# The first block's transfers through DRAM: outer steps of 16, 32 or 64 partitions over rows of 1 KB, and all spills ahead of the three fills

## The chip, the core and the metric

The kernel runs on one core of a Trainium2 chip. The metric is the device time of one execution in microseconds (us). The core has a matrix engine (TensorE, PE in the profile), three elementwise engines (VectorE = DVE, ScalarE = ACT, GpSimd = POOL) and 16 DMA engines, which all DMA queues share. DMAs are issued here by SyncE (SP) and by ScalarE; "SPq" and "ACTq" in the profile are the issuing instructions. Each engine works through its own instructions in order, and an issuing engine that waits on a semaphore holds up everything behind it.

## The reference

The input is a batch of 8 sequences of 3008 rows by 256 features. A two-dimensional Fourier transform is taken of each, its real part kept, and every row then goes through a two-layer network with 2048 hidden features.

```
X = np.fft.fft(x, axis=1)
X = np.fft.fft(X, axis=2)
x = X.real.reshape(B * S, D)
h = x @ w_in
g = h * (1.0 / (1.0 + np.exp(-1.702 * h)))
return g @ w_out
```

## The kernel before

A sequence is transformed in two stages, with 3008 = 47 x 64. Stage one multiplies, for each of 64 residues, 47 rows by a table of cosines and sines; stage two combines the residues. Between the two the data change layout: stage one leaves a frequency on a partition, stage two needs the residue there. The kernel does that through DRAM: a "spill" writes stage one's rows to a scratch tensor, a "fill" reads them back into the tile `t4` with another assignment of rows to partitions. The feature transform is folded into the weights. After stage two, the network runs in steps: 8 sequences, 3 blocks each, 16 steps a block, almost all of it on PE.

The first sequence has a path of its own, in a setup of some 120 us, since nothing can be hidden behind earlier work. It goes as follows, in the order written out by hand.

- `load_first` and `load_mirror` bring in the first sequence; a loop over `i` from 0 to 7 folds it on DVE (`fold_first`), multiplies on PE (`mix_first`, line 335) and copies the result on ACT (line 337) into one of four tiles `made[0]` to `made[3]`, two values of `i` for each tile. A tile has two halves c, at partitions 0 and 64; in each half the first 16 partitions belong to the first of stage two's three blocks.
- `spill_first(k, engines)` (line 343) writes those 16 partitions of both halves of `made[k]` to the scratch tensor `Tf`: two DMAs of 16 partitions by four rows of 1 KB, 64 KB each. Half 0 goes on SP's queue; half 1 goes on ACT's queue, but for k = 2, where both go on SP's.
- `fill_first` (line 347) reads `Tf` back into `t4`, in three DMAs, all on SP's queue: partitions 1, 3, 5 and so on (64 of them, 256 KB, called fill 1 below), partitions 2, 6, 10 and so on (32 of them, 128 KB, fill 2), and partitions 0, 4, 8 and so on (32, 128 KB, fill 3). Fill 1 needs the spills of k = 0 and 1, fill 2 those of k = 2, fill 3 those of k = 3.
- Each row that a fill moves is 4 KB, all four of a partition's values in one piece. For that the table `w0` has its first 16 columns of every residue reordered, and the scratch tensor is written so that the four values stand side by side. On the DRAM side a fill's access pattern begins with a step of 4, on the SBUF side with a step of 64 or 32 partitions.
- `spill_rest` (line 352) writes the other 32 frequencies to another scratch tensor, `Td`; `fill(0, 4, NG)` (line 374) reads them much later, for the other two blocks.

Once `t4` is filled, `rotate(0, 0, 4)` works on one column of it with PE (tile `psr`, line 196), `stage2(0, 0)` multiplies it on PE (line 394), DVE transposes the result (line 401), and `first_row(0)` follows on PE and ACT (tile `psf`, lines 532 and 533).

Meanwhile the weights are prepared. They arrive as 64-bit numbers in eight loads of 1 MB (`load_in`, line 427, and `load_out`, line 432), and each goes through ACT (`sizes`, line 445, and `low`, line 455), POOL (`clamp`, line 451), DVE (`high`, lines 470 and 471) and POOL again (lines 483 and 491). `load_in(0)` is on SP's queue, `load_in(1)` on ACT's, issued when i is 5; `load_out(0)` and the others are on SP's queue, after the three fills. In ACT's own order, `sizes` of `out0` comes after `first_row(0)`.

SP's order around the change, before: the two halves of `load_in(0)`, the small matrices (line 904), the spills of k = 0 and 1, fill 1, the two spills of k = 2, the spill of k = 3, fills 2 and 3, `load_out(0)`, `spill_rest`. The DMAs of SP and ACT use eight completion counters in turn, so a DMA also waits until the one issued eight places before it, in the order of the program, has landed.

Of the kernel before, what the change touches and what calls it, by code (L numbers as in the profile page):

```python
# [27 lines left out]
F32 = mybir.dt.float32  # L28
# [7 lines left out]
NJ = NB // 2  # L36
NM = 48
# [10 lines left out]
def view(ap, offset, *dims):  # L48
    return bass.AP(ap.tensor, ap.offset + offset, [list(d) for d in dims])
# [6 lines left out]
def kp(u, a):  # L56

    n, i = a // 4, 2 * (a % 4) + u
    return 8 * n + i if n else 7 - i


def tables(S, D):

    assert S == NA * NB and D == 256
    H = D // 2
    ks = np.array([kp(u, a) for a in range(NG) for u in range(NU)])
    s = NB * np.arange(NA)[:, None, None] + np.arange(NB)[None, :, None]
    angle = 2.0 * np.pi * ((s * ks) % S) / S
    cos, sin = np.cos(angle), np.sin(angle)
    w1 = np.zeros((NA, NJ + 3, NG * NU, 2))  # L70
    w1[:, 1:NJ, :, 0], w1[:, 1:NJ, :, 1] = cos[:, 1:NJ], sin[:, 1:NJ]
    e0, o0, e1, o1 = ENDS
    w1[:, e0, :, 0], w1[:, o0, :, 0], w1[:, e1, :, 1], w1[:, o1, :, 1] = cos[:, 0], sin[:, 0], cos[:, NJ], sin[:, NJ]


    w0 = np.zeros((128, NJ + 1, NG * NU, 2))
    low, high, back = w0[0:2 * NA:2], np.zeros((NA, NJ + 1, NG * NU, 2)), NJ - np.arange(1, NJ)
    low[:] = w1[:, :NJ + 1]
    high[:, 1:NJ, :, 0], high[:, 1:NJ, :, 1] = cos[:, NJ + back], -sin[:, NJ + back]
    high[:, e0, :, 1], high[:, o0, :, 1] = cos[:, NJ], -sin[:, NJ]  # L80
    w0[33:33 + 2 * NA:2] = high
    w0 = w0.reshape(128, NJ + 1, NM)
    w0[:, :, :16] = w0[:, :, :16].reshape(128, NJ + 1, 4, 4).swapaxes(2, 3).reshape(128, NJ + 1, 16)
    sign = np.ones((128, 4))
    sign[33:33 + 2 * NA:2] = -1.0

    c, q = np.divmod(np.arange(NJ), 16)
    m2 = []
    h, y = np.array([0, 2, 1, 3])[np.arange(NJ) % 4], np.arange(NJ) // 4
    at = 16 * (y // 4) + 4 * h + y % 4  # L90
    for jj in np.where(c, 16 + q, np.where(q, 16 - q, 0))[at], 4 * (q // 2) + 2 * (q % 2) + c:
# [12 lines left out]

    m, d = np.arange(D)[:, None], np.arange(H)[None, :]
    phi = 2.0 * np.pi * ((m * d) % D) / D
    cd = np.stack([np.cos(phi), -np.sin(phi)], 1)
    cd[:, 1, 0] = 1.0 - 2.0 * (np.arange(D) % 2)
    cd = cd.reshape(2, H, 2, NB, 2).transpose(1, 0, 2, 4, 3)
    small = [t.reshape(128, -1) for t in (*m2, rot, cd)]  # L110
    pad = 64 - NM
    ends = 2.0 * np.pi * ((NJ * np.arange(NM)[:, None] * ks) % S) / S
    w1 = np.pad(w1[:, :NJ + 1], ((0, NM - NA), (0, 0), (0, 0), (0, 0)))
    w1[:, 0], w1[:, NJ] = 0.0, 0.0
    for c in range(2):
# [8 lines left out]
def kernel(ctx: ExitStack, tc, x, w_in, w_out, tab1, tab2, out):  # L124
    nc = tc.nc
    B, S, D = x.shape
# [16 lines left out]
    Xr = [nc.dram_tensor(f"Xr{b}", (NA, NJ, D), F32, kind="Internal").ap() for b in range(B)]  # L143
    Nd = nc.dram_tensor("Nd", (B * NBLK, 512), F32, kind="Internal").ap()
    Tk = nc.dram_tensor("Tk", (B * NBLK * NF, 1), F32, kind="Internal").ap()
    Tf = nc.dram_tensor("Tf", (NJ * 4, 4 * D), F32, kind="Internal").ap()
    Td = [nc.dram_tensor(f"Td{b}", (NG * 128, D), F32, kind="Internal").ap() for b in range(B)]

    w1 = const.tile([128, (NJ + 1) * NM + 64 - NM], F32, tag="w1", name="w1")
# [48 lines left out]
    t4t, pqt, nbt = {}, {}, {}  # L198
# [112 lines left out]
    def fold_first(g):  # L311

        t, e = xt[:, 4 * g:4 * g + 4, :], room[g]
        fwd, rev = t[:, :, 1:H], free(t, D - 1, [D, 4], [-1, H - 1])
        nc.vector.tensor_tensor(e[:, :, 0:H - 1], fwd, rev, op=ALU.subtract)
        if g not in BY_PE:
            nc.vector.tensor_tensor(fwd, fwd, rev, op=ALU.add)

    def mix_first(i):

        ps, ns = bank("ps1"), (2 * i + 2, 2 * i + 1) if i < 7 else (0, 15)
        for at, n in enumerate(ns):
            todo = [], []
            for c, slot in enumerate((n, NJ - n if n else 16)):
                o = ps[64 * c:64 * c + 64, at * D:(at + 1) * D]
                even, odd_ = (w[:, k * NM:k * NM + 64] for w, k in ((w0, slot), (odd, slot or NJ)))
                todo[c].append((o[:, H + 1:], odd_, room[slot // 4][:, slot % 4, 0:H - 1], True, True))
                folded = slot // 4 not in BY_PE
                todo[c].append((o[:, 0:H + 1], even, xt[:, slot, 0:H + 1], True, folded))
                if not folded:  # L330
                    todo[c].append((o[:, 1:H], even, free(xt[:, slot], D - 1, [-1, H - 1]), False, True))
            for k in range(3):
                for c in range(2):
                    for o, w, rhs, first_, end in todo[c][k:k + 1]:
                        nc.tensor.matmul(o, lhsT=w, rhs=rhs, start=first_, stop=end, skip_group_check=True)
        to = 2 - i % 2 * 2
        nc.scalar.copy(made[i // 2][:, to:to + 2, :].rearrange("p j d -> p (j d)"), ps[:])

    PLACE = 3, 1, 2, 0

    def spill_first(k, engines):
        for c, eng in enumerate(engines):
            eng.dma_start(out=view(Tf, (PLACE[k] + 16 * c) * 16 * D, [D, 16], [64 * D, 4], [1, D]), in_=made[k][64 * c:64 * c + 16])

    def fill_first(at, apart):
        one, n = t4t[0][at:at + 1], NJ // apart
        nc.sync.dma_start(out=bass.AP(one.tensor, one.offset, [[apart * t4t[0][:].ap[0][0], 4 * n], [1, 4 * D]]),
                          in_=view(Tf, at * 16 * D, [4 * D, 4], [apart * 16 * D, n], [1, 4 * D]))

    def spill_rest(k):  # L350
        for c in range(2):
            nc.sync.dma_start(out=view(Td[0], (NJ * 16 + 16 * c + PLACE[k]) * D, [NJ * D, NM - 16], [4 * D, 4], [1, D]),
                              in_=made[k][64 * c + 16:64 * c + NM])

    def load_matrices():
# [514 lines left out]
    odd, w0 = flat[:, 0:n0], flat[:, 6176:6176 + n0 + 4]  # L870
# [4 lines left out]
    made = rooms[1:] + [pqp.tile([128, 4, D], F32, tag="pq", name="e")[:]]  # L875
# [5 lines left out]
    for lo, hi in (28, 32), (24, 28), (20, 24), (8, 12), (12, 20):  # L881
# [10 lines left out]
                      in_=view(tab1, 0, [tab1.shape[1], 128], [28 * NM, 2], [1, ends]))  # L892
# [16 lines left out]
    for i, need in enumerate(((0, 7), (1,), (6,), (2,), (5,), (3,), (4,), ())):  # L909
        for g in need:  # L910
            fold_first(g)
        mix_first(i)
        if i == 0:
            warm(3)
            spare[:] = spare[5:] + spare[:5]
        if i % 2:
            spill_first(i // 2, (nc.sync, nc.sync if i == 5 else nc.scalar))
        if i == 5:
            load_in(1, nc.scalar)
        if i == 3:  # L920
            fill_first(1, 2)
        if i == 7:
            fill_first(PLACE[2], 4)
        if i == 3:
            sizes(in0, nc.scalar, 0, 512)
            clamp(in0, 0, 512)
        if i in (4, 7):
            low(in0, 512 * (i // 7), 512)
        if i == 6:
            sizes(in0, nc.vector, 512, 512)  # L930
            clamp(in0, 512, 512)
            for h0 in (0, 512):
                high(in0, h0, 512)
    fill_first(PLACE[3], 4)
    load_out(0, nc.sync)
    spill_rest(0)
    load_in(2, nc.sync)
    for k in range(1, 4):
        spill_rest(k)
# [35 lines left out]
    n = len(steps)  # L975
# [17 lines left out]
    for b in range(B):  # L993
# [43 lines left out]
    for t in range(n + LAG):  # L1037
# [14 lines left out]
        else:  # L1052
# [13 lines left out]
            one, other = (t - LAG, (1, 2, 4, 7)), (t - LAG - 1, (5, 6, 3))  # L1066
# [70 lines left out]
```

## Time and profile before

| | us |
|---|---|
| median of three runs | 1852.49 |
| lowest and highest | 1852.17 and 1854.78 |
| the profiled execution's own time | 1852.52 |
| its span in the trace | 1850.7 |
| PE busy | 1827.8 (99% of the span) |
| DVE, ACT, POOL busy | 1481.1, 1138.7, 997.7 |
| HBM read and written | 65.07 MB and 48.05 MB, 61 GB/s over the span |

Between the span and the execution's own time lie 1.8 us. Times in the trace count from the span's start. The profile's chain of waits follows the work that ended last back to the start, each piece to what released it. In the view of stages, a row gives the length of a stretch, then for each engine its busy time and the instructions in it, then the granted clock of TensorE (1.00 is full), the mean busy share of the 16 DMA engines, and GB/s. In the timeline, a row has start, length, engine, line, operation and count, and in brackets how long the engine had been idle and what ended that.

### The profile page before, as it was taken

The page shows a single profiled execution, that of the slowest core. Times are in us where ns is not written, and L with a number is a line of the kernel's source. Part 1 is how long each engine was busy: PE and PEld are TensorE (multiplying, and loading weights), DVE is VectorE, ACT ScalarE, POOL GpSimd, SP SyncE. Part 2 cuts the span into 40 slices and gives each one's busy share as a digit, 9 for nine tenths or more (in the row PEclk, how much of TensorE's full clock was granted, in tenths as well). Part 3 has the DMA queues.
Part 4 walks back from the last instruction along what each step waited for, and adds up shares of the span by engine and source line. Part 5 has one row for each costly group of instructions (what it writes and reads, how often), then busy time and mean ns, then how long its engine had stood idle before and what let it go on. Part 6 is the DMA issues. An engine that isn't in the chain of part 4 may idle for free.

```text
span 1850.7 us, 55846 instructions
## 1 busy us (share of the span) xinstructions
PE 1827.8 (99%) x23650; PEld 1399.4 (76%) x23650; DVE 1481.1 (80%) x1930; ACT 1138.7 (62%) x2231; POOL 997.7 (54%) x1068
## 2 busy tenths in 40 slices
PE   7999999999999999999999999999999999999998
PEld 4677777777777777777777777777777877778776
DVE  5888888887888878887888778877888788878874
ACT  3656665666567666666665666666666666556663
POOL 3695556654556546565455644656446654444442
PEclk8999999999999999999999999999999999999999
DMA  8731340213312142211512115021241111100001
GB/s 250 204 72 32 80 74 22 61 26 92 62 28 55 37 107 37 60 32 36 114 20 66 35 51 98 19 74 27 65 79 24 36 26 56 30 19 13 23 19 24
DMA packets 151605, 105.95 MB, mean 57 GB/s; under 512 B 106193, under 2 KB 132819, under 8 KB 150796
## 3 DMA queue, kind: packets, MB, share of 16 engines
q1 hardware_dynamic: 148140, 99.35, 22.5%
q8 instruction: 186, 3.05, 0.7%
q10 hardware_dynamic: 3216, 3.03, 0.6%
q14 instruction: 63, 0.52, 0.1%
HBM read 65.07 MB, written 48.05 MB: 61 GB/s over the span
## 4 chain that ended last, share of the span: by engine, by line
PE 93%; POOL 2%; DVE 2%; DMA 2%; issue 1%; ACT 0%; SPq 0%; DVEq 0%; POOLq 0%; ACTq 0%
PE x L196 34%; PE o L196 26%; PE low L717 25%; PE o L717 4%; PE ps L273 2%; PE ps L394 1%; DMA xt<-in_x_dram 1%; DMA Tf<-big 1%; POOL wo L491 0%; PE po L196 0%; DMA t<-Tf 0%; DVE big L471 0%; POOL wo L509 0%; POOL wst L483 0%; POOL big L648 0%
## 5 line engine op out<-in xcount | busy, mean ns | idle before, releaser
L648 POOL TENSOR_TENSOR big<-big 128x256 f32<-128x256 f32 (+1 forms) x376 | 352.7, 938 | 786.0 <-ACT big L640 666.2
L196 PE MATMUL x<-pq,wcs 128*64 128x256 f32 (+1 forms) x6016 | 768.8, 376 | 1.3 <-ACT g L630 0.8
L196 PE MATMUL o<-big,wo 128*64 128x256 f32 (+1 forms) x4800 | 621.1, 375 | 0.5 <-DVE big L655 0.5
L196 PEld LDWEIGHTS x<-pq,wcs 128*64 128x64 f32 x6016 | 414.3, 137 | 180.7 <-issue 15.6
L630 ACT ACTIVATE g<-x 128x512 f32<-128x512 f32 (+1 forms) x376 | 221.7, 590 | 380.3 <-PE x L196 379.2
L196 PEld LDWEIGHTS o<-big,wo 128*64 128x64 f32 x4800 | 341.5, 137 | 147.1 <-DVE big L655 0.9
L649 POOL TENSOR_TENSOR big<-big 128x256 f32<-128x256 f32 (+1 forms) x376 | 411.3, 1094 | 0.0
L637 DVE TENSOR_TENSOR big<-g,x 128x512 f32<-128x512 f32 (+1 forms) x376 | 250.9, 667 | 182.3 <-ACT big L633 182.0
L618 ACT ACTIVATE x<-nb,af 128x256 f32<-128x256 f32 (+1 forms) x752 | 353.0, 469 | 70.4 <-DVE pq L401 57.3
L717 PE MATMUL low<-big 128*64 128x128 f32 (+1 forms) x5888 | 381.4, 270 | 0.0
L717 PEld LDWEIGHTS low<-big 128*64 128x64 f32 x5888 | 336.8, 137 | 28.2
L633 ACT ACTIVATE big<-x 128x512 f32<-128x512 f32 (+1 forms) x376 | 219.2, 583 | 120.4 <-PE x L196 110.4
L679 DVE TENSOR_TENSOR big<-big 128x1024 f32<-128x1024 f32 (+1 forms) x184 | 235.5, 1280 | 65.6 <-PE low L717 42.8
L640 ACT ACTIVATE big<-big 128x512 f32<-128x512 f32 (+1 forms) x376 | 231.6, 616 | 35.7 <-DVE big L637 33.4
L717 PE MATMUL low<-big,wo 128*64 128x128 f32 (+1 forms) x2944 | 220.2, 270 | 0.1
L681 DVE TENSOR_TENSOR big<-big 128x512 f32<-128x512 f32 (+1 forms) x184 | 179.6, 976 | 16.3 <-DVE big L679 0.5
L683 DVE TENSOR_TENSOR big<-big 128x512 f32<-128x512 f32 (+1 forms) x184 | 184.6, 1003 | 0.0
L717 PEld LDWEIGHTS low<-big,wo 128*64 128x64 f32 x2944 | 171.9, 137 | 4.1 <-DVE big L683 0.5
L656 DVE TENSOR_TENSOR big<-big 128x512 f32<-128x512 f32 (+1 forms) x188 | 143.3, 762 | 6.5
L655 DVE TENSOR_TENSOR big<-big 128x512 f32<-128x512 f32 (+1 forms) x188 | 131.3, 698 | 3.5 <-POOL big L648 3.5
L819 DVE TENSOR_TENSOR big<-big,low 128x512 f32<-128x512 f32 (+3 forms) x184 | 109.0, 609 | 3.8
L717 PEld LDWEIGHTS o<-big,wo 128*64 128x64 f32 x1472 | 92.3, 137 | 24.9
(112 smaller groups left out, 1106.7 us busy)
## 6 DMA issues: line engine op xcount, KB each, us to landing
out_dram<-os SPq DMA_DIRECT2D x284, 64.0 KB
Td<-xt SPq DMA_DIRECT2D x56, 192.0 KB
t<-Td SPq DMA_DIRECT2D x21, 512.0 KB
xt<-in_x_dram SPq DMA_DIRECT2D x14, 512.0 KB
xt<-Xr SPq DMA_DIRECT2D x14, 512.0 KB
nb<-Nd SPq DMA_DIRECT2D x23, 256.0 KB
out_dram<-os SPq DMA_DIRECT2D x96, 56.0 KB
Xr<-in_x_dram SPq DMA_DIRECT2D x7, 752.0 KB
```

The source lines that it names most:

```text
L196: nc.tensor.matmul(out[c0:c0 + 64], lhsT=lhs[:, c0:c0 + 64], rhs=rhs, skip_group_check=True, **how)
L618: nc.scalar.activation(x[:, i * 256:i * 256 + n], nbt[b, blk][:, hh * 256:hh * 256 + n], ACTF.Copy, scale=af1[:, f:f + 1])
L630: nc.scalar.activation(two(g[:], n), two(xb[t][:], n), ACTF.Copy, scale=2.0)
L633: nc.scalar.activation(front(t), two(xb[t][:], width(t)), ACTF.Gelu_apprx_sigmoid)
L637: nc.vector.tensor_tensor(back(t), two(gt.pop(t)[:], n), two(xb.pop(t)[:], n), op=ALU.subtract)
L640: nc.scalar.activation(back(t), back(t), ACTF.Gelu_apprx_sigmoid)
L648: eng.tensor_tensor(right(t, S1, n), left(t, A21, n), right(t, A22, n), op=ALU.add)
L649: eng.tensor_tensor(left(t, S3, n), left(t, A11, n), left(t, A21, n), op=ALU.subtract)
L679: nc.vector.tensor_tensor(free(big[:], SUM, *both_), free(big[:], from11 + w, *twice), free(big[:], from11, [at_right(t, 0) + w - from11, ...
L681: nc.vector.tensor_tensor(s2, a11, s1, op=ALU.subtract)
L683: nc.vector.tensor_tensor(s4, a12, s2, op=ALU.subtract)
L717: nc.tensor.matmul(o, lhsT=lhs, rhs=rhs, start=first_in, stop=(p == NP - 2), skip_group_check=True)
```

## The change

The four rows that belong to a partition are no longer side by side in `Tf`, and the columns of `w0` are no longer reordered. A spill of k = 0 or 1 writes rows of 1 KB at a distance of two rows, 16 partitions by four; a spill of k = 2 or 3 writes four rows in one piece, 4 KB from each of 16 partitions. A fill reads four rows of 1 KB for each partition, and on both of its sides the access pattern begins with the partitions, 64 for fill 1 and 32 for fills 2 and 3. So fill 1 has 256 rows of 1 KB for 64 of 4 KB, and fills 2 and 3 have 128 each for 32.

Fill 1 moves from i = 3 to i = 7: on SP's queue it now stands behind the three spills of k = 2 and 3. SP's order becomes: spills of k = 0 and 1, two spills of k = 2, the spill of k = 3, fill 1, fill 2, fill 3, `load_out(0)`. The order of every other engine is the same. With the counters taken in turn, the two spills of k = 2 now wait for the first half of `load_in(0)` and for the spill of k = 0 on ACT's queue, and SP's spill of k = 3 waits for the small matrices.

```diff
-    w0 = w0.reshape(128, NJ + 1, NM)
-    w0[:, :, :16] = w0[:, :, :16].reshape(128, NJ + 1, 4, 4).swapaxes(2, 3).reshape(128, NJ + 1, 16)
...
-    Tf = nc.dram_tensor("Tf", (NJ * 4, 4 * D), F32, kind="Internal").ap()
+    Tf = nc.dram_tensor("Tf", (NJ * 16, D), F32, kind="Internal").ap()
...
-    PLACE = 3, 1, 2, 0
-
     def spill_first(k, engines):
+        base, by = (0, 2) if k < 2 else (128 * k, 1)
         for c, eng in enumerate(engines):
-            eng.dma_start(out=view(Tf, (PLACE[k] + 16 * c) * 16 * D, [D, 16], [64 * D, 4], [1, D]), in_=made[k][64 * c:64 * c + 16])
-
-    def fill_first(at, apart):
-        one, n = t4t[0][at:at + 1], NJ // apart
-        nc.sync.dma_start(out=bass.AP(one.tensor, one.offset, [[apart * t4t[0][:].ap[0][0], 4 * n], [1, 4 * D]]),
-                          in_=view(Tf, at * 16 * D, [4 * D, 4], [apart * 16 * D, n], [1, 4 * D]))
+            to = base + 4 * c * by + (1 - k if k < 2 else 0)
+            eng.dma_start(out=view(Tf, to * D, [8 * by * D, 16], [by * D, 4], [1, D]), in_=made[k][64 * c:64 * c + 16])
+
+    def fill_first(base, at, apart):
+        one, n = t4t[0][at:at + 1], 4 * NJ // apart
+        nc.sync.dma_start(out=bass.AP(one.tensor, one.offset, [[apart * t4t[0][:].ap[0][0], n], [D, 4], [1, D]]),
+                          in_=view(Tf, base * D, [D, n], [n * D, 4], [1, D]))
...
-        if i == 3:
-            fill_first(1, 2)
         if i == 7:
-            fill_first(PLACE[2], 4)
+            fill_first(0, 1, 2)
+            fill_first(256, 2, 4)
...
-    fill_first(PLACE[3], 4)
+    fill_first(384, 0, 4)
```

`spill_rest` keeps its places, with the tuple of `PLACE` written out in it.

More of the change, by code (lines that the diff above doesn't have):

```diff
@@ L337, in mix_first @@
         nc.scalar.copy(made[i // 2][:, to:to + 2, :].rearrange("p j d -> p (j d)"), ps[:])
-    PLACE = 3, 1, 2, 0
     def spill_first(k, engines):
+        base, by = (0, 2) if k < 2 else (128 * k, 1)
         for c, eng in enumerate(engines):
-            eng.dma_start(out=view(Tf, (PLACE[k] + 16 * c) * 16 * D, [D, 16], [64 * D, 4], [1, D]), in_=made[k][64 * c:64 * c + 16])
-    def fill_first(at, apart):
-        one, n = t4t[0][at:at + 1], NJ // apart
-        nc.sync.dma_start(out=bass.AP(one.tensor, one.offset, [[apart * t4t[0][:].ap[0][0], 4 * n], [1, 4 * D]]),
-                          in_=view(Tf, at * 16 * D, [4 * D, 4], [apart * 16 * D, n], [1, 4 * D]))
+            to = base + 4 * c * by + (1 - k if k < 2 else 0)
[4 more added lines that the diff above has]
+                          in_=view(Tf, base * D, [D, n], [n * D, 4], [1, D]))
     def spill_rest(k):
         for c in range(2):
-            nc.sync.dma_start(out=view(Td[0], (NJ * 16 + 16 * c + PLACE[k]) * D, [NJ * D, NM - 16], [4 * D, 4], [1, D]),
+            nc.sync.dma_start(out=view(Td[0], (NJ * 16 + 16 * c + (3, 1, 2, 0)[k]) * D, [NJ * D, NM - 16], [4 * D, 4], [1, D]),
                               in_=made[k][64 * c + 16:64 * c + NM])
```

## The prediction

> **What bounds the kernel now.** I read the page's totals first, then the chain of waits through the setup, then the issues of SyncE and the busy share of the DMA engines in the same stretch.
>
> ```profile
> span 1850.7 us, 55846 instructions
> ...
> PE 93%; POOL 2%; DVE 2%; DMA 2%; issue 1%; ACT 0%; SPq 0%; DVEq 0%; POOLq 0%; ACTq 0%
> ```
>
> PE carries 93% of the chain, and none of that work is edited. What the change can move is the 2% of DMA, all of it in the setup. If the setup ends earlier by some us, the rows of matrix work that follow in a fixed order start earlier by as much, and so does the end. The chain there (start, length, what):
>
> ```profile
> 19.53 4.95 DMA Tf<-big
> ...
> 25.73 5.19 DMA Tf<-big
> ...
> 31.66 5.27 DMA t<-Tf
> 36.93 0.25 issue
> 37.17 0.38 PE psr L196 x4
> 37.56 1.89 PE ps L394 x64
> 39.45 0.97 PE psf L196 x16
> ...
> 40.68 1.04 ACT big L445
> ...
> 42.95 1.76 DVE big L470
> ```
>
> Three transfers in a row set the time: a spill of k = 1, a spill of k = 2, fill 3. Fill 3 lands at 36.93, and only then do PE, ACT (which has `first_row` ahead of the sizes of `out0`, L445), POOL and DVE go on with the weights. From 42.95 the chain is DVE and POOL in their own order. PE had nothing for 8 us:
>
> ```profile
> 25.16 3.90 PE L196 MATMUL psw<-wst,small 128*64 128x512 f32 x16 [0.96 <-POOL wst L483]
> 37.17 0.38 PE L196 MATMUL psr<-t,small 128*64 128x4 f32 x4 [8.12 <-DMA t<-Tf]
> ```
>
> Why the transfers take that long is seen in SyncE's issues and the DMA engines' share (stretch, its length, engines, granted clock, DMA share, GB/s):
>
> ```profile
> 18.56 1.28 SPq L343 DMA_DIRECT2D Tf<-big  x2
> 24.55 0.67 SPq L347 DMA_DIRECT2D t<-Tf  x1
> 25.29 0.87 SPq L343 DMA_DIRECT2D Tf<-big  x2
> 26.20 0.43 SPq L343 DMA_DIRECT2D Tf<-e  x1
> 30.99 1.17 SPq L347 DMA_DIRECT2D t<-Tf  x2
> 32.22 0.44 SPq L432 DMA_DIRECT2D big<-in_moe_w_out_dram  x1
> ```
> ```profile
> 28.10:29.60 1.50, 0.96 (x6) 0.07 (x2) 0.80 (x1) 1.44 (x3) 1.19 (x2) 1.00 0.27 109
> 31.00:32.00 1.00, 0.00 (x0) 0.00 (x0) 0.00 (x0) 0.00 (x0) 0.77 (x1) 1.00 0.00 0
> 32.00:33.50 1.50, 0.00 (x0) 0.00 (x0) 0.00 (x0) 0.00 (x0) 0.00 (x0) 0.50 0.20 30
> 33.50:36.00 2.50, 0.00 (x0) 0.00 (x0) 0.00 (x0) 0.00 (x0) 0.00 (x0) 0.50 0.88 254
> ```
>
> SyncE stood before fill 1 from 19.84 to 24.55, with the spills of k = 2 behind it. From 28.10 to 29.60 fill 1 is almost alone in flight, and the share is 0.27 at 109 GB/s: about a quarter of the 16 engines works at full rate and the rest has nothing. The spills issued behind it at 25.73 wait 5.19 us, which I read as their parts on those four engines standing behind fill 1's. From 32.00 to 33.50 fills 2 and 3 are alone and again stay under a quarter, 0.20. In both, the side in DRAM begins with a step of 4.
>
> The Trainium skill has a rule for this ("DMA: Bandwidth & Descriptors", section "Why a DMA increments its semaphore by 16 and not by 1"): a DMA issued by SyncE or ScalarE runs on the largest number of engines up to 16 that divides the outermost sizes of both its sides. By that rule the old fills run on 4 and the new ones (64 and 32 on both sides) on 16. The trace agrees with its first half, 0.27 of 16 engines being 4.3.
>
> **The change part by part.** The order of the table's columns changes numbers, not instructions: 0. The spills of k = 0 and 1 keep 64 rows of 1 KB; those of k = 2 and 3 become 16 rows of 4 KB: 0, between a loss of 0.2 and a gain of 0.2 us, since 64 KB at the 254 GB/s above is 0.3 us in any shape.
>
> *The issues.* The two spills of k = 2 no longer stand behind fill 1. What else they need:
>
> ```profile
> 16.75 0.37 ACTq L343 DMA_DIRECT2D Tf<-big  x1
> ...
> 20.44 0.69 ACT L445 ACTIVATE big<-big 128x512 f32<-128x512 f32 x1 [0.94 <-DMA big<-in_moe_w_in_dram]
> ...
> 22.11 0.58 ACT L337 COPY big<-ps 128x512 f32<-128x512 f32 x1
> 22.57 1.19 ACT L337 COPY e<-ps 128x512 f32<-128x512 f32 x2
> 23.80 0.32 ACTq L343 DMA_DIRECT2D Tf<-e  x1
> 27.37 1.20 ACT L455 ACTIVATE big<-big 128x1024 uint32<-128x1024 uint32 x1 [2.55 <-DMA big<-in_moe_w_in_dram]
> ```
>
> Their data are there at 22.69, so they go out at 22.7 and 23.1 instead of 25.29. Their new waits on counters ask for the first half of `load_in(0)`, which landed at 20.44, and for the spill issued at 16.75, which with the 4.95 us of the chain's crowded spill lands at 21.7: both over before. SyncE's spill of k = 3 needs the copy that ends at 23.76, and by its counter the small matrices. The trace shows of these only that the spill at 25.73, which had the same wait, was not held; so it goes out between 23.8 and 25.7. I take 24.2, and fill 1, which still needs the spill that landed at 24.48, at 24.7 instead of 24.55 (24.6 to 26.2 by the ends). Moving fill 1 behind three issues costs it 0.1 us, and it doesn't end the chain. Fill 2 needs the spills of 22.7 and 23.1: with the 4.95 us of the chain's crowded spill they land by 28.1, and I take 26.5.
>
> Fill 3 needs the last spill on ACT's queue, issued at 23.80 behind the 1 MB of `load_in(1)`, which lands at 27.37. So it lands between 27.4 and 31.1 (before, fill 3 left SyncE at 31.66, some 0.6 behind fill 2). I take 27.9: right behind that load, with 0.2 us for its own 64 KB and 0.3 us for fill 1, now in the crowd. Fill 3 goes out at 28.0 instead of 31.66.
>
> *The fill itself.* No row before shows a fill from `Tf` on all engines. The nearest is the fill from `Td` in the steady part, 512 KB in 512 rows of 1 KB, with 128 partitions outermost and nothing beside it:
>
> ```profile
> 209.62 0.38 SPq L374 DMA_DIRECT2D t<-Td  x1
> ...
> 209.60:210.20 0.60, 0.60 (x10) 0.38 (x8) 0.32 (x1) 0.00 (x0) 0.00 (x0) 1.00 0.00 0
> 210.20:211.40 1.20, 1.20 (x26) 1.20 (x24) 0.63 (x1) 1.01 (x2) 0.00 (x0) 1.00 0.43 39
> 211.40:213.20 1.80, 1.80 (x22) 1.22 (x20) 1.62 (x2) 1.22 (x4) 1.62 (x2) 1.00 0.76 265
> 213.20:213.80 0.60, 0.60 (x9) 0.38 (x7) 0.23 (x1) 0.33 (x1) 0.52 (x1) 1.00 0.11 27
> ```
>
> Traffic begins 0.6 us after the issue, creeps for 1.2 at 39 GB/s, runs for 1.8 at 265 and ends some 0.2 later; with 0.3 for the signal that is 4.1. A quarter of the bytes needs a quarter of the 1.8 + 0.2: 0.6 + 1.2 + 0.5 + 0.3 = 2.6 us, and 0.4 for fill 2's tail ahead of it, 3.0. The ends are 1.8 (no slow start) and the 5.27 of before. Fill 3 lands at 28.0 + 3.0 = 31.0 instead of 36.93: **5.9 us earlier**.
>
> *What is late next.* PE, ACT, POOL and DVE then follow as before: `psr` at 31.3, L445 at 34.8. It also needs `load_out(0)`, 1 MB, which goes out after fill 3, at 28.6. A load of that kind by itself:
>
> ```profile
> 55.48 9.00 SPq L432 DMA_DIRECT2D big<-in_moe_w_out_dram  x2
> ...
> 59.00:60.00 1.00, 1.00 (x12) 0.83 (x10) 1.00 (x2) 1.00 (x2) 0.21 (x1) 1.00 0.58 238
> ```
>
> It is through by 59.6 to 60, 4.1 to 4.5 us after its issue, so `out0` is there by 33.4, ahead of 34.8. Later loads have room: `load_in(3)` goes out at 46.04 and its first reader on ACT starts at 58.50,
>
> ```profile
> 46.04 0.50 SPq L427 DMA_DIRECT2D big<-in_moe_w_in_dram  x1
> 58.50 1.21 ACT L445 ACTIVATE big<-big 128x1024 f32<-128x1024 f32 x1
> ```
>
> 12.5 us for a 1 MB load. If that cover were gone, each us of lateness would come off the gain.
>
> *Sum.* 0 + 0 + 3.66 (fill 3's issue, 31.66 to 28.0) + 2.27 (its length, 5.27 to 3.0) = 5.9. The profiled execution took 1852.52, 1.8 more than its span, and lies 0.03 above the median of the runs: 1852.5 - 5.9 = **1846.6 us**.
>
> One more thing can add to it. In the rows above the granted clock is 1.00 until 32.00 and 0.50 after, PE having stood since 29.06, and `psr` to `psf` took 3.25 us (37.17 to 40.42) at that clock. With PE back at 31.3 the clock may not fall; then that stretch takes 1.6, L445 starts at 33.5 (when `out0` is there too), and the time is 1845.4. I keep the lower clock, since at 32.0 the stretch before it would still be mostly idle.
>
> The Trainium skill ("TensorE: Matmul & The Clock Gate", section "Part 1: The HAM clock gate") says the clock falls after an idle window of about 3.4 us. By that rule the new gap, 2.3 us, would be too short, and the sum would be the 1845.4; no run so far shows such a gap here.
>
> **The rivals.**
>
> *The fills stay narrow.* If the quarter share has another cause than the step of 4 (the source tensor, the partition steps of 2 and 4), a fill keeps its 5.27 us, and the change gives the order alone: 3.7 us, 1848.9. For it: the steps of partitions stay. Against: the fill from `Td` reaches 0.76.
>
> *`load_out(0)` becomes the bound.* Before, a spill of SyncE waited for it until 39.70:
>
> ```profile
> 39.70 0.88 SPq L352 DMA_DIRECT2D Td<-e  x2
> ```
>
> That is 7.5 us after 32.22. If it takes 7.5 us again, from 28.6, L445 starts at 36.2 instead of 40.68: 4.5 us, 1848.0. For it: `spill_rest` still crowds in behind it. Against: part of the 7.5 was the narrow fills ahead of it on a quarter of the engines.
>
> *Slower, by rows four times as many.* The three fills have 512 rows for 128, and all now stand behind every spill. In their slow start the old fills' rows were dear, whatever their size:
>
> ```profile
> DMA packets 11, 0.05 MB, mean 30 GB/s; under 512 B 0, under 2 KB 0, under 8 KB 11
> ```
>
> From 32.00 to 33.50, 11 packets took 0.20 x 16 x 1.5 = 4.8 engine-us, 0.44 us each. If a row of 1 KB costs that throughout, 32 rows on each of 16 engines take 14.1 us from 25.7 on, and with 0.3 for the signal fill 3 lands at 40.1: 3.2 us later, 1855.7. It turns slower above (36.6 - 25.7)/32 = 0.34 us a row. Against: from 211.40 on, 1 KB rows run at 265 GB/s.
>
> **How the numbers follow.** Forecast 0.76, its own range 1845.2 to 1847.9 (fill 3 at 27.7 with the full clock; 28.5 with 3.8 us); narrow fills 0.09; `load_out(0)` the bound 0.10; slower 0.05. The range of 1844.6 to 1849.4 takes in the forecast, the two smaller gains, and at its low end a fill of 1.8 us, where `out0`, there at 32.7 at the earliest, becomes the bound. Left out are the slower case and mishaps beyond the bounds. About 0.2%, 3.7 us, is what a measurement of this kernel tells from no change. Faster by more: the forecast, and most of the second smaller gain, 0.84. Within: most of the narrow fills, 0.10. Slower: 0.06, with a little for a late spill of k = 3.
>
> **What would show it.** SyncE's issues: spills of k = 2 near 22.7, fill 1 near 24.7, fill 3 near 28.0. While a fill is alone, a DMA share well over 0.25. `psr` near 31.3, L445 near 34.8, then the same chain on DVE and POOL, 6 us earlier up to the first steps on PE, and the busy time of PE unchanged. Wrong would be: a fill that holds 0.25 for long; L445 ended by a DMA; or a gain at L445 that has shrunk by the first steps.

## The result and the profile after

| | before | after |
|---|---|---|
| median of 12 runs each, in turn on one chip | 1852.5 | 1847.99 |
| lowest and highest | 1851.96 and 1855.03 | 1846.24 and 1850.13 |
| the profiled execution's own time | 1852.52 | 1847.86 |
| its span | 1850.7 | 1846.1 |

The ratio is 0.9974 with a 95% interval of 0.9965 to 0.9983: the kernel is faster by 4.5 us by the medians, and between 3.1 and 6.5 by the interval. The forecast was 1846.6, in a range of 1844.6 to 1849.4. The time lies in the range and the sign is right, but the gain is 1.4 us short of the 5.9, and the profile puts this shortage down to one step of the working, the length of `load_out(0)`.

The chain of waits of the changed kernel through the setup (start, length, what); lines of the kernel have numbers two lower than before:

```profile
22.87 0.32 SPq L341
...
23.23 4.50 DMA Tf<-big
...
27.75 0.61 SPq L345
...
28.45 0.58 SPq L345
...
29.08 6.99 DMA big<-in_moe_w_out_dram
...
36.09 4.07 DMA Td<-e
```

Fill 3 is no longer in the chain as a wait. It goes out at 28.45 (31.66 before), and what follows it in the chain is only its issue; then comes `load_out(0)`, 6.99 us from 29.08. The `Td<-e` piece is a DMA of `spill_rest` that waits for the load by its counter; it lands at 40.16, level with DVE's own step. What the engines waited for is plainer in the timeline, PE and then ACT (start, length, engine, line, what, and in brackets the idle time before and what ended it):

```profile
31.04 0.28 PE L194 MATMUL psr<-t,small 128*64 128x4 f32 x4 [1.82 <-DMA t<-Tf]
31.26 1.20 PE L392 MATMUL ps<-t,small 64*32 64x128 f32 x64
32.38 0.74 PE L194 MATMUL psf<-twos,wcs 128*64 128x1 f32 x16
```
```profile
33.17 0.16 ACT L530 COPY af<-psf 128x4 f32<-128x4 f32 x1 [1.64 <-PE psf L194]
33.23 0.18 ACT L531 ACTIVATE af<-psf 128x4 f32<-128x4 f32 x1
36.09 1.13 ACT L443 ACTIVATE big<-big 128x1024 f32<-128x1024 f32 x1 [2.69 <-DMA big<-in_moe_w_out_dram]
```

`psr` starts 6.13 us earlier than before (37.17 to 31.04), and ACT's copy of `psf` starts 7.27 us earlier (33.17). ACT is through with `first_row` at 33.41 and then stands for 2.69 us until the load of `out0` has landed. Before, it went straight on:

```profile
40.44 0.16 ACT L532 COPY af<-psf 128x4 f32<-128x4 f32 x1 [2.68 <-PE psf L196]
...
40.57 1.15 ACT L445 ACTIVATE big<-big 128x1024 f32<-128x1024 f32 x1
```

So `sizes` of `out0` starts at 36.09 instead of 40.57 (the chain, which cuts off the overlap with the instruction before, had 40.68): 4.48 us, which is 7.27 less 2.69 and less the overlap of 0.1. DVE then shows what remains of it:

```profile
38.38 1.75 DVE L468 TENSOR_SCALAR big<-big 128x1024 uint32<-128x1024 uint32 x1 [3.41 <-POOL big L449]
```

42.95 before, 38.38 after: 4.57 us, and the span is shorter by 4.6. Nothing is gained or lost from there to the end. PE's busy time is 1827.0 for 1827.8.

The DMA engines while fills 2 and 3 are in flight and the load begins (stretch, length, engines, granted clock, DMA share, GB/s):

```profile
29.00:29.50 0.50, 0.22 (x2) 0.00 (x0) 0.50 (x1) 0.30 (x2) 0.37 (x1) 1.00 0.52 162
...
30.00:31.00 1.00, 0.00 (x0) 0.00 (x0) 0.38 (x1) 0.00 (x0) 0.47 (x1) 1.00 1.27 234
...
32.00:33.00 1.00, 1.00 (x48) 0.78 (x31) 0.51 (x2) 0.00 (x0) 0.00 (x0) 0.88 0.96 393
...
33.50:36.00 2.50, 2.34 (x12) 1.39 (x14) 1.44 (x4) 0.00 (x0) 0.00 (x0) 0.50 1.01 357
```

From 29.00 to 29.50 the share is 0.52, where the old fills stayed at 0.20 to 0.27. From 32 on the engines are full at 357 to 393 GB/s: the load has company. (A share above 1.00, as from 30.00 to 31.00, cannot be meant literally; shares are not read to the last tenth here.)

The packed trace also records each step by which a DMA's completion counter rises. Before, the counter of fill 3 rose, after one early step at 32.58, in four steps at its landing (36.70, 36.72, 36.89, 36.93); now it rises in sixteen, from 30.56 to 30.90. Of the sixteen steps of the spill that went out at 25.73 before, twelve had come by 27.90 and the other four came from 30.39 to 30.93, right behind the four of fill 1 (30.04 to 30.58). Read as one step for each engine, this is four engines under an old fill and sixteen under a new one, and it shows the old fill 1 holding up, on its four engines alone, what stood behind it. For the load of `out0` in the changed kernel, fifteen steps came from 34.03 to 34.58 and the sixteenth at 36.07.

### The profile page after: what moved, and what is told of

Read it like the earlier page. It is cut to its first block, busy times and chain, and to the rows that moved or that the text cites. A ratio compares the mean times of both kernels' runs of the same rounds, so it can differ in the third digit from the quotient of the medians.

```text
span 1846.1 us, 55847 instructions
## 1 busy us (share of the span) xinstructions
PE 1827.0 (99%) x23650; PEld 1397.5 (76%) x23650; DVE 1480.6 (80%) x1930; ACT 1139.2 (62%) x2231; POOL 999.6 (54%) x1068
## 4 chain that ended last, share of the span: by engine, by line
PE 93%; POOL 2%; DMA 2%; DVE 2%; issue 1%; ACT 0%; SPq 0%; ACTq 0%; DVEq 0%; POOLq 0%
PE x L194 34%; PE o L194 26%; PE low L715 25%; PE o L715 4%; PE ps L271 2%; PE ps L392 1%; DMA xt<-in_x_dram 0%; POOL wo L489 0%; DMA big<-in_moe_w_in_dram 0%; DMA big<-in_moe_w_out_dram 0%; PE po L194 0%; DVE big L469 0%; POOL wo L507 0%; POOL wst L481 0%; POOL big L646 0%
```

## The experiments

The runs stand in groups by question. Each was timed in turn with the kernel before on one chip, and a median is compared through that ratio; "shift" is how much earlier `sizes` of `out0` starts in the timeline than the 40.57 of before (4.48 in the changed kernel).

### Width or order

**order_only** keeps the old shapes and moves fill 1 alone.

```diff
-        if i == 3:
-            fill_first(1, 2)
         if i == 7:
+            fill_first(1, 2)
             fill_first(PLACE[2], 4)
```

> The old shapes of spills and fills, in the new order (fill 1 behind all spills). Theory A (the first 1 MB load of w_out, issued behind fill 3, now ends the wait of ScalarE for the sizes of out0): fill 3 goes out near 28.4; the three fills still share a quarter of the DMA engines, 32 rows of 4 KB on each, and fill 3 lands near 32.7; the w_out load goes out near 29.1, its parts on those four engines stand behind the fills, and it lands at 36 to 36.5; the sizes of out0 start there, so that the order alone already has 4.2 to 4.7 us, 1848. Theory B (the width of the fills brings most, the order little): fill 3 lands after 34.5, the sizes start after 38.5, gain under 2 us, 1850.5 or more.

Measured: 1849.99, ratio 0.9984 (0.9974 to 0.9994), 2.6 us by the medians; the profile has a shift of 1.30. The chain of this run:

```profile
23.45 6.53 DMA Tf<-big
...
30.64 5.10 DMA t<-Tf
...
35.88 0.38 PE psr L196 x4
36.26 1.89 PE ps L394 x64
38.15 0.97 PE psf L196 x16
...
39.38 1.05 ACT big L445
```

Fill 3 is as long as before (5.10, before 5.27), and it goes out at 30.64, not at 28.0: the spill of k = 2 took 6.53 us although it stood ahead of fill 1 on its queue.

**order_only2** is the same kernel a second time.

> The run with the order alone (old shapes, all spills ahead of the fills) a second time, since in its first profile the spills of k = 2 were held on two late DMA engines until 29.97. Theory A (an old fill keeps its 5 us of length on a quarter of the engines, and its issue is what varies): fill 3 again takes 5.0 to 5.3 us from issue to landing; with the spills of k = 2 in by 27.8 it goes out at 28.5 to 30 and lands by 33.5 to 35, sizes of out0 at 38 to 39.4, so 1.3 to 2.7 us of gain in the profile and 1849.8 to 1851 as the median. Theory B (the width was not the matter, the order is worth the forecast's 3.7): fill 3 out at 28.0, landing by 33.0, sizes at 37.0, 1848.8.

Measured: 1850.87, 0.9991 (0.9982 to 1.0); in the profile the spill took 5.74, fill 3 went out at 30.51 and took 5.55, `sizes` at 39.59, a shift of 1.0. So the order by itself is worth 1.0 to 1.3 us in the profiles and 1.5 to 2.6 in the medians, not 3.7; the interval of this second run reaches no change. The DMA engines of this run with the narrow fills in flight:

```profile
29.00:29.50 0.50, 0.50 (x4) 0.14 (x2) 0.01 (x1) 0.01 (x1) 0.00 (x0) 1.00 0.27 109
...
30.00:31.00 1.00, 0.14 (x2) 0.00 (x0) 0.27 (x2) 1.00 (x2) 0.72 (x2) 1.00 0.24 98
```

It is the quarter share of before again.

**shape_only** takes the new shapes and leaves fill 1 at i = 3, ahead of the spills of k = 2.

```diff
         if i == 7:
-            fill_first(0, 1, 2)
             fill_first(256, 2, 4)
...
+        if i == 3:
+            fill_first(0, 1, 2)
```

> The new shapes, with fill 1 at its old place ahead of the spills of k = 2 and 3. Theory A: fill 1 goes out near 24.5 and is through by 28 on all engines, the spills behind it land near 28.3 instead of 31, fill 3 goes out near 29 and lands near 31.5, the w_out load goes out near 29.6 and lands near 36.5, gain about 4 us, 1848.4; each half of the change alone then has nearly all of its gain. Theory B: width brings most, the same 4 us here, but with the order alone under 2. A third reading (the shapes cost something and the order alone pays): the spills land near 31 as before, gain under 1.5 us.

Measured: 1848.22, 0.9977 (0.9967 to 0.9986), a shift of 4.6: all of the change's gain. Its chain:

```profile
25.96 2.99 DMA Tf<-big
...
29.72 2.89 DMA t<-Tf
...
32.86 0.28 PE psr L194 x4
33.15 1.60 PE ps L392 x63
34.75 0.97 PE psf L194 x16
```

A spill of k = 2 behind fill 1 now takes 2.99 us, where before it took 5.19 behind a narrow one. With the counters of the result above, this confirms the reading that narrow fills hold up what stands behind them. Fill 3 lands later than in the changed kernel and PE runs at half clock, but `load_out(0)` went out at 30.36 and was in at 35.92 here, so the sum is the same: the better order of the changed kernel brings `psr` 1.8 us sooner and finds the load not there.

**rows4k** tells the row's size from the outer step: the fills read 4 KB in one piece for each partition, as before, but with 64 or 32 outermost. They read other rows than a partition's own.

```diff
-        nc.sync.dma_start(out=bass.AP(one.tensor, one.offset, [[apart * t4t[0][:].ap[0][0], n], [D, 4], [1, D]]),
-                          in_=view(Tf, base * D, [D, n], [n * D, 4], [1, D]))
+        nc.sync.dma_start(out=bass.AP(one.tensor, one.offset, [[apart * t4t[0][:].ap[0][0], n], [1, 4 * D]]),
+                          in_=view(Tf, base * D, [4 * D, n], [1, 4 * D]))
```

> The changed kernel with fills that read one piece of 4 KB for each partition, partitions outermost on both sides (64 and 32), instead of four rows of 1 KB; a partition gets other rows of the scratch tensor than its own, so the first block's values are not the reference's. If the outermost size of 4 made the old fills narrow: these are as wide as the changed kernel's, fill 3 lands 2.2 to 3 us after its issue, and the time is that of the changed kernel, 1848. If rows of 4 KB made them narrow: the DMA share stays at 0.25 while fill 1 runs, fill 3 lands 3.5 to 5 us after its issue, 1849 to 1850.

Measured: 1848.07, 0.9977 (0.9967 to 0.9986). Fill 3 went out at 30.06 and landed at 32.43, and PE went on at once:

```profile
32.56 0.28 PE L194 MATMUL psr<-t,small 128*64 128x4 f32 x4 [2.15 <-DMA t<-Tf]
```

That is 2.4 us with rows of 4 KB, as with rows of 1 KB, and again sixteen counter steps (32.07 to 32.43). The load behind it took 5.92 us, and the shift is 4.0. What made the old fills 5.3 us was the outermost size of 4; the size of the rows is not seen in the time. This is the rule cited in the prediction (the Trainium skill, "DMA: Bandwidth & Descriptors", section "Why a DMA increments its semaphore by 16 and not by 1"), and the runs agree with both halves of it: four steps at the landing of an old fill, sixteen for a new one of either row size.

### Is `load_out(0)` the bound?

**after2** is the changed kernel a second time.

> The changed kernel once more, for a second look at the engine that came last. If one DMA engine is late by a fixed cause, the wait of ScalarE for the w_out load ends 1 to 2 us behind psf again, with sizes of out0 at 35 to 36.2; if that was chance, the sizes start between 33.3 and 35. The time stays at 1847.5 to 1848.5.

Measured: 1847.8, 0.9977 (0.9968 to 0.9987). ACT again:

```profile
33.41 0.16 ACT L530 COPY af<-psf 128x4 f32<-128x4 f32 x1 [1.53 <-PE psf L194]
...
36.01 1.16 ACT L443 ACTIVATE big<-big 128x1024 f32<-128x1024 f32 x1 [2.36 <-DMA big<-in_moe_w_out_dram]
```

The load took 6.62 us from 29.37. Its lateness is not an accident of one execution.

**half_out0** brings only half of that load's bytes; POOL sets the other half of the tile to a constant.

```diff
     def load_out(n, eng):
         t = raw["out", n] = ring("raw").bitcast(U32).rearrange("p (n w) -> p n w", w=2)
+        if n == 0:
+            eng.dma_start(out=t[:].rearrange("p (f n) w -> p f (n w)", f=4)[:, 0:2],
+                          in_=w_out[0:512, :].bitcast(U32).rearrange("(p f) n -> p f n", p=128)[:, 0:2])
+            return
```

> The changed kernel with only half of the first w_out load's bytes (two of its four rows of each partition; the rest of the raw tile is a constant, so a quarter of w_out is not used and the output is not the reference's). Theory A (that load's landing holds the sizes of out0): 512 KB land 1.5 to 3 us sooner, 33 to 34.5, the sizes start right behind psf or that landing, 33.3 to 34.6 instead of 36.1, and the whole run gains as much, 1845.5 to 1846.5. Rival (what is missing from the forecast is lost further on): the sizes start as early, but DVE's high part of out0 or the first steps come no earlier than in the changed kernel, 1848.

Measured: 1847.24, 0.9973 (0.9963 to 0.9983), the span 1844.9. Its ACT:

```profile
33.42 0.16 ACT L534 COPY af<-psf 128x4 f32<-128x4 f32 x1 [1.53 <-PE psf L194]
...
34.41 1.15 ACT L447 ACTIVATE big<-big 128x1024 f32<-128x1024 f32 x1 [0.76 <-DMA big<-in_moe_w_out_dram]
```

Half the bytes landed in 5.07 us, and `sizes` moved from 36.09 to 34.41, still ended by that load, and the span by 1.2 us. So in the profiles the load's landing sets the start of `sizes` after the change. The time is less clear: 1847.24 is above the 1845.5 to 1846.5 that was expected, and only 0.6 under the changed kernel beside it (after2, 1847.8), which the intervals don't tell from no change. The run also shows that 5.07 us is there for 0.5 MB: the load's length is not its bytes alone.

### Can the load be had earlier?

**out_act** sends it on ACT's queue behind the last spill, ahead of all fills.

```diff
         if i == 7:
+            load_out(0, nc.scalar)
             fill_first(0, 1, 2)
...
-    load_out(0, nc.sync)
```

> The changed kernel with the first w_out load issued on ScalarE's queue, right behind its last spill, instead of on SyncE's behind fill 3. Theory A: issued near 24.4 it lands near 32, ahead of the end of psf near 33.2; the sizes of out0 start at 33.3 to 33.6, not held by a DMA, 7 us earlier than before, and the time is 1845 to 1846. Rival (the missing 1.3 us of the forecast are lost after the sizes of out0, not to this load): the sizes start earlier, but the first steps on PE do not, and the time stays at 1848. Second rival: the load in the crowd delays the last spill or fill 3 by about as much, sizes at 35 or later, 1847.

Measured: 1849.14, 0.9979 (0.997 to 0.9989), with a shift of 2.9. The load was in by 34.09, but now others were late:

```profile
18.19 8.58 DMA small<-in_tab_dram
26.84 3.49 DMA Tf<-e
30.38 4.98 DMA t<-Tf
...
35.49 0.28 PE psr L194 x4
```

SyncE's spill of k = 3, which by its counter waits for the small matrices, only went out at 26.84. That is not the load's doing: the small matrices were in at 26.77, and the load itself went out only at 26.97. Fill 3 took 4.98 us for 2.5 with 1 MB ahead of it; fifteen of its counter's sixteen steps had come by 33.72, 3.3 us after its issue, and the last came at 35.36.

**out_sp** sends it on SyncE's queue, between the last spill and fill 1.

```diff
         if i == 7:
+            load_out(0, nc.sync)
             fill_first(0, 1, 2)
...
-    load_out(0, nc.sync)
```

> The changed kernel with the first w_out load on SyncE's queue ahead of the three fills instead of behind them. Theory A: issued near 24.3 it lands near 30 to 31; the fills' rows stand behind it on every engine, and the second w_in load and the spill behind it are slowed, so fill 3 lands near 32.3, psr starts near 32.6 and the sizes of out0 near 34.7: gain 6 us, 1846.5. Rival as for the other placement: no better than the changed kernel's 1848.

Measured: 1847.97, 0.9974 (0.9964 to 0.9984). The load ran from 24.09 to 31.11, and the bound changed hands:

```profile
29.05 3.48 DMA t<-Tf
...
32.67 0.38 PE psr L194 x4
33.05 1.89 PE ps L392 x64
34.94 0.97 PE psf L194 x16
...
36.17 1.05 ACT big L443
```

Fill 3 took a microsecond more and PE found the clock at 0.50, so that `psr` to `psf` took 3.24 us for the 2.08 of the changed kernel: the shift is 4.5 again.

**out_sp_warm** adds seven matrix products that nobody reads behind `fold_w(0)`, to hold the clock.

```diff
     fold_w(0)
+    warm(7, "o0", small)
     rotate(0, 0, 4, nc.scalar.copy)
```

> The first w_out load ahead of the fills on SyncE's queue, and seven more 128x512 matmuls on PE behind the first weight fold, in the time in which PE waits for fill 3. If, with that load out of the way, fill 3 and the half clock after PE's idle time set the sizes of out0: the clock stays at 1.00, psr to psf take 1.7 us instead of 3.2, the sizes start near 34.7 instead of 36.2, and the time is 1846 to 1846.7. Rival: the extra matmuls end behind fill 3's landing and delay psr by as much as the clock gives: 1848. Second rival: the clock falls all the same, 1848.

Measured: 1852.09, 1.0 (0.999 to 1.0009). They were mis-sized:

```profile
31.37 6.28 PE L363 MATMUL o<-small 128*128 128x512 f32 x14
37.58 0.28 PE L194 MATMUL psr<-t,small 128*64 128x4 f32 x4
37.79 1.20 PE L393 MATMUL ps<-t,small 64*32 64x128 f32 x64
38.92 0.63 PE L194 MATMUL psf<-twos,wcs 128*64 128x1 f32 x16
```

Seven products are 14 passes and 0.9 us each. The clock held (1.20 us for L393 and 0.63 for `psf`; at half clock the timeline of out_sp has 1.96 and 1.02), but `psr` stood behind them.

**out_sp_warm3** is the same with three.

```diff
-    warm(7, "o0", small)
+    warm(3, "o0", small)
```

> Leaves nothing of the result out; adds three matrix products of 128x512 that nobody reads, behind the last matrix product on the first weights. With load_out(0) ahead of the three fills on SyncE's queue, the load is in by about 31 and fill 3 by about 32.5; PE then found the clock at one half, and psr to psf took 3.4 us for 1.9. By the run with seven such products each takes 0.9 us, so three fill about 2.7 us of PE's gap from 29.4 and end by 32.1, before fill 3 lands. Theory A (landing of load_out(0) bounds the change; taken away, the bound is fill 3 and the clock): the clock stays at 1.00 until psr, psr at 32.6, end of psf at 34.5, sizes of out0 at 34.5 to 35.0 instead of 40.68, and the time 1846.3 to 1847, 1 to 1.5 us under the changed kernel. Theory B (the load's earlier issue only moves the crowd to the fills): fill 3 lands at 33.5 or later, sizes of out0 at 35.5 to 36.2, 1847.5 to 1848.

Measured in the profile: the products end at 32.3, `psr` at 32.55 right at fill 3's landing, the clock at 1.00 throughout, and ACT no longer waits for any DMA:

```profile
34.57 0.16 ACT L531 COPY af<-psf 128x4 f32<-128x4 f32 x1 [1.53 <-PE psf L194]
...
34.69 1.16 ACT L444 ACTIVATE big<-big 128x1024 f32<-128x1024 f32 x1
```

`sizes` starts at 34.69, a shift of 5.9, the forecast's own. Yet the span is 1845.5, only 0.6 below the changed kernel's, and the time 1847.45, 0.9978 (0.9969 to 0.9987). Of the 1.4 us gained at `sizes`, POOL's next step gives back 0.4 (1.45 us for 1.04), so that DVE's step of 38.38 starts at 37.43; another 0.35 is gone by the end. Against the changed kernel, this is not to be told from no change: the 1846.3 to 1847 expected was not reached.

### Why the load takes 7 us

**rest_held** puts a DMA of 4 bytes from the load's tile behind it, so that `spill_rest` and `load_in(2)` cannot go out before the load is in.

```diff
     load_out(0, nc.sync)
+    nc.sync.dma_start(out=Dm[:], in_=raw[out0][0:1, 0:1, 1])
     spill_rest(0)
```

> The changed kernel with one more DMA on SyncE's queue, of 4 bytes from the tile of load_out(0) to a scratch word in DRAM, right behind that load. It cannot go out before the load has landed, so spill_rest and load_in(2), which stand behind it, cannot share the engines with the load. Theory A (load_out(0) takes 7 us because of what is issued behind it): alone it takes the 4.1 to 4.5 us of the row at 55.48, from 29.1 to 33.2 to 33.6, sizes of out0 at 33.6 instead of 36.09, ended by the load or by af; the setup's steps shift by 6.5 to 7 us against the kernel before, and the time is 1846 if the work held back has room (spill_rest 4 us later, fill from Td at 44 to 46 instead of 42.52). Theory B (the load is long by itself, for its start or for a late engine): 29.1 to 35.5 or later, sizes of out0 at 35.5 to 36.2, and 1848 or more, since the rest is held for nothing.

Measured: 1848.7, 0.9978 (0.9969 to 0.9988). This execution had fallen 1.6 us behind before the load went out, so lengths are compared: the load took 5.84 us, from 30.72 to 36.56, and `sizes` came at 36.59, ended by it. The engines meanwhile:

```profile
31.00:32.00 1.00, 0.00 (x0) 0.00 (x0) 0.78 (x2) 0.02 (x1) 0.04 (x1) 1.00 0.74 218
32.00:33.00 1.00, 0.34 (x12) 0.35 (x20) 0.00 (x0) 0.02 (x1) 1.00 (x1) 1.00 0.95 166
33.00:34.00 1.00, 1.00 (x65) 0.79 (x61) 0.00 (x0) 0.15 (x1) 0.23 (x1) 1.00 0.90 377
...
35.50:36.00 0.50, 0.50 (x4) 0.30 (x4) 0.47 (x3) 0.00 (x0) 0.00 (x0) 0.50 0.08 33
36.00:36.25 0.25, 0.25 (x4) 0.07 (x2) 0.25 (x1) 0.00 (x0) 0.00 (x0) 0.50 0.00 0
```

It starts slowly: until 33 the engines carry the fills and the load's beginning, at a share near 1 but at 166 GB/s for 377 a microsecond later. And it ends slowly: by 35.50 nearly all bytes have moved, and the signal comes at 36.56. The DMA queues of the same stretch:

```profile
q8 instruction: 1, 0.02, 1.0%
```

One packet of the instruction queue, and 1.0% of 16 engines over 5.9 us is 0.94 us on one engine. In the trace it runs from 35.47 to 36.45. Of the load's counter steps, fifteen had come by 36.03 and the last came at 36.56, just behind that packet.

**in2_last** moves `load_in(2)` alone behind all of `spill_rest`.

```diff
-    spill_rest(0)
-    load_in(2, nc.sync)
-    for k in range(1, 4):
+    for k in range(4):
         spill_rest(k)
+    load_in(2, nc.sync)
```

> The changed kernel with load_in(2) behind all eight DMAs of spill_rest instead of behind the first two. By the counters taken in turn, the last of these waits for load_out(0), so the 1 MB of load_in(2) goes out behind that load, at 34 to 36 instead of 30.7; six of the eight DMAs of spill_rest, 0.8 MB, still crowd in. Theory A (the load is held by what shares the engines, in proportion to the bytes): 29.1 to 34.0 to 35.0, sizes of out0 at 34.1 to 35.1, a shift of 5.6 to 6.5 us, 1846.5 to 1847. Theory B (long by itself): sizes of out0 at 35.5 to 36.2, 1848. If load_in(2) then is late for its reader on ACT, at 50 in the changed kernel, the shift shrinks from there on.

Measured: 1848.78, 0.9977 (0.9968 to 0.9986); the load took 6.63 us from 29.47, `sizes` at 36.13. Theory A is out: with nothing behind it the load is far from 4.1 to 4.5 us. How much the crowd costs is not settled, since the load took 5.56 us in shape_only and 5.92 in rows4k with the whole crowd behind it, 6.62 and 6.99 in the changed kernel; the 5.84 and 6.63 of these two runs lie among them. And holding the rest back is no better a kernel.

The counter steps of the load divide its length further. In the table, the last column is the packet of the instruction queue that came nearest, each of 16 KB; times are in us from the span's start:

| run | load out | 15th step | 16th step | length | packet |
|---|---|---|---|---|---|
| changed kernel | 29.08 | 34.58 | 36.07 | 6.99 | 34.84 to 35.78 |
| after2 | 29.37 | 35.75 | 35.98 | 6.62 | 35.07 to 35.95 |
| rest_held | 30.72 | 36.03 | 36.56 | 5.84 | 35.47 to 36.45 |
| shape_only | 30.36 | 35.90 | 35.92 | 5.56 | 36.31 to 37.26 |
| rows4k | 30.66 | 36.36 | 36.58 | 5.92 | 36.69 to 37.64 |
| in2_last | 29.47 | 35.87 | 36.11 | 6.63 | 36.39 to 37.34 |

In the first three the packet came before the load was in, and the load's last step followed its end by 0.29 us or less; in after2 fourteen steps had come by 34.82 and two were late. In the other three the packet came after the load, and no step stands alone. So the longest load, 6.99 us, is 5.50 for fifteen parts and 1.49 for one late one. That the packet holds up that one engine is an inference: the trace doesn't say on which engine a packet runs, and in out_act the last step of fill 3 came 1.6 us late with the last such packet over at 24.02. What makes fifteen parts take between 5.3 and 6.4 us in these runs stays open.

## Why the prediction came out so

**The parts without cost.** As predicted: no work on PE was added (1827.0 for 1827.8), and the shapes of the spills are not seen anywhere in the setup.

**The issues.** Right to some tenths: the first spill of k = 2 at 22.87 (forecast 22.7), the spill of k = 3 at 23.92 (24.2), fill 1 at 24.32 (24.7), fill 3 at 28.45 (28.0). One wait on the way was longer than taken: fill 2 stood for the second spill of k = 2 until 27.73, for 26.5, and fill 3 went out right behind it. It cost little, since the spill of k = 3 that fill 3 needs landed only at 28.26 (27.9).

**The fill.** Right to half a microsecond: forecast 3.0 us, measured 2.45 (28.45 to 30.90), and `psr` starts at 31.04 for 31.3. The price worked out from the fill from `Td` held; its 0.3 us for the signal had no row, but that fill's last counter step, at 213.78, is 4.16 us after its issue, for the 4.1 taken. "The fills stay narrow" is out by shape_only and rows4k, and "slower, by rows four times as many" too: 1 KB rows cost what 4 KB rows do.

**What the two terms were put down to.** Here the working was wrong though its sum was right: fill 3 went out 3.21 us earlier and took 2.82 less, 6.03 for the forecast's 5.93. The forecast gave the earlier issue to the order and the shorter length to the width, and priced the order alone at 1848.9. But with the width alone (shape_only) fill 3 already went out 1.94 us earlier, since the spills of k = 2 no longer stood behind a narrow fill. With the order alone it went out at 30.5 to 30.6, and the kernel took 1850.0 and 1850.9: the second spill of k = 2 took 6.53 and 5.74 us (4.50 in the changed kernel). Why is not shown. It isn't the four engines of fill 1, which would make four steps late: in order_only fourteen of that spill's steps had come by 27.77 and two came at 29.23 and 29.97, in order_only2 fifteen by 28.98 and one at 29.84. In runs with wide fills the same spill took up to 5.63 us (rows4k) and 6.40 (out_sp_warm).

**The clock.** The forecast kept the lower clock, 3.25 us from `psr` to the end of `psf`. It took 2.08: the clock fell only between 32 and 33, granted 0.88 there. By the rule of the Trainium skill that was weighed ("TensorE: Matmul & The Clock Gate", section "Part 1: The HAM clock gate") a stand of 1.82 us should not bring a fall at all; here it fell at 32.76, 1.7 us after PE was at work again, and in the second execution of the same kernel it was 1.00 until 41.68. The traces agree with the rule's 3.4 us, though not with a wholly idle window as the condition. In every profile here the stretches at one clock, but for those that the profile's ends cut, last whole multiples of 3.41 us: in the changed kernel 1.00 from 5.45 to 32.76 (8 times) and 0.50 to 39.58 (twice), before 1.00 from 8.10 to 32.00 (7 times). So the clock changes only at the ends of such periods, and these lie elsewhere in each execution: the forecast's 32.0 was the place of one of them in one execution. In the period that ended with the fall, 29.34 to 32.76, PE was busy for 1.72 us; in after2 it was busy for 1.48 from 28.02 to 31.44, and the clock stayed. What counts as idle thus stays open, and whether `psr` finds the full clock was not to be known beforehand. With 1845.4 as the sum for a full clock, `sizes` was due at 33.4 by ACT's own row, and only the load was missing.

**The step that failed: "so `out0` is there by 33.4".** It was there at 36.07. The load went out at 29.08 (forecast 28.6) and took 6.99 us, for the 4.1 to 4.5 read from a load at 55.48 with no fills and no spills around it. That turned a cover of 1.4 us into a wait of 2.69. Three things make the difference. The 4.1 to 4.5 is where that load's bytes end in the view of stages; its counter's last step came at 60.36, 4.88 us after its issue. Beside fills and spills, fifteen of sixteen parts took 5.50. The last part took another 1.49.

The rival "`load_out(0)` becomes the bound" had carried over the 7.5 us of before and came to 36.2, a gain of 4.5 and 1848.0; the profile has 36.09, 4.6 in the span, and a median of 1847.99. It was given 0.10 because "part of the 7.5 was the narrow fills ahead of it". That objection was sound: before, twelve steps of the load had come by 38.40, 6.2 us after its issue, and four came from 39.35 to 39.69. In the changed kernel that delay is gone and another, of one part, has come in its place, so that the rival's hit to a tenth is partly luck; so is it that the full clock, which the forecast didn't count on, brought nothing because the load was later still. In the six profiles with wide fills ahead of the whole 1 MB, it still took 5.6 to 7.0 us, whatever stood behind it. So the row in place, long as it was, was nearer the truth than the cleaner row from elsewhere, though not for all of its reasons.

## What to carry to other kernels

Where a setup waits for transfers, cost the next transfer in line by its length in that place and crowd, up to the last step of its counter and not to its last bytes, and compare its landing with the time that the change would free. See to the outermost sizes of a DMA's two sides before its order in the queue: with an outermost size of 4, a fill stayed on four engines here and held up what stood behind it. When two or three waits end within some 2 us of each other, removing one is worth only the distance to the next.

## What the runs showed that was not expected

- A load's signal can come about a microsecond after almost all of its bytes: in the run with the rest held back, the share was 0.08 from 35.50 and 0.00 from 36.00, the last counter step came at 36.56, and a 16 KB packet of the instruction queue ran from 35.47 to 36.45. In the changed kernel one step of sixteen came 1.49 us behind the others, 0.29 behind such a packet.
- Busy DMA engines are not fast ones: at a share of 0.95 they moved 166 GB/s while a load began beside fills, and 377 at 0.90 a microsecond later.
- The matrix clock fell after PE had been back at work for 1.7 us in one execution, and not in that stretch in another of the same kernel; it changes only at whole multiples of 3.41 us, whose place differs between executions.
- A product of 128x512 in f32 cost 0.9 us as a filler at the full clock, in two passes (6.28 us for seven, 2.84 for three).
